# Chunk 0's output as seven block products, and two gate units moved later, to the values of batch 1

The chip is one Trainium2 chip, of which one core is used. The metric is the device time of one execution in microseconds. The kernel before takes 329.07 us (median of three, 328.59 to 329.21; a fourth, the traced one, took 329.17).

## The reference

```python
# q, k, v: (8 batches, 8 heads, 576, 64)
k_p = k.reshape(B, H, 72, 8, D).mean(axis=3)        # keys and values pooled by 8
v_p = v.reshape(B, H, 72, 8, D).mean(axis=3)
attn = softmax(q @ k_p.T / 8)
x = (attn @ v_p) as (4608 tokens, 512)
h = relu(x @ w_gate) * (x @ w_val)                  # (4608, 1536)
out = h @ w_out                                     # (4608, 512)
```

## The kernel before

The 4608 tokens go through in nine chunks of 512. Attention of one batch is woven into the gate and value matmuls of an earlier chunk. A batch has 576 tokens, so chunk 1 needs a rest of batch 0 and four of batch 1's five pieces. Names used below: `a[f]` and `z[f]` are gate and value of the first and second half of chunk 0's tokens; `V[t]` computes piece t of batch 1's values; `x[t]` transposes that piece into `x_T`, the input of the gates; `gv[f]` is a gate and value unit of a later chunk; `kpT0l` and `kpT0u` are the two halves into which a batch's transposed keys are copied, and `px` holds attention values on their way to the transpose. PSUM is the memory in which the results of this kernel's matmuls land; its three pools below hold four, three and one bank, and a pool hands its banks out in turn.

```python
ps_mm  = ctx.enter_context(tc.tile_pool(name="ps_mm", bufs=4, space=PSUM))   # gates, values of w, transposes
ps_at  = ctx.enter_context(tc.tile_pool(name="ps_at", bufs=3, space=PSUM))   # scores, attention values
ps_acc = ctx.enter_context(tc.tile_pool(name="ps_acc", bufs=1, space=PSUM))  # block products
...
def k_transposes(b):
    ps = ps_mm.tile([P, KJ + 1, KROWS], F16, name="mm_ps", tag="mm_ps")
    k_windows(b, ps, 0, KJ + 1)
    eng = nc.scalar if b > 2 else nc.vector
    k_evacuate(b, ps, False, eng)                     # kpT0l
    k_evacuate(b, ps, True, eng)                      # kpT0u
...
def back(b, t, eng):                                  # x[t]
    ...
    for g in range(NG):
        nc.tensor.transpose(out=ps[:, g, :n], in_=x[:, g, :], identity=ident16[:n, :n])
    eng.copy(dst, ps[:, :, :n])                       # into x_T
...
def out_rows(c, ts, eng=None):                        # chunk 0's output, plainly
    cell = []
    def part(lo, hi):
        if not cell:
            cell.append(ps_mm.tile([P, DM], F32, name="mm_ps", tag="mm_ps"))
        for fo in range(lo, hi):                      # 6 matmuls of 512 columns
            nc.tensor.matmul(out=cell[0], lhsT=h_tiles[c][:, fo, ts*P:(ts+1)*P], rhs=wo_sb[:, fo, :], ...)
        ...                                           # after the second half: copy and store
    return [lambda: part(0, n_fo // 2), lambda: part(n_fo // 2, n_fo)]
```

Later chunks use a Strassen-like form (`out_products`): the 2x2 blocks of h and of w_out need seven products in place of eight, for which VectorE makes sums of blocks of h (`sum`) and, once, of w_out (`weight_sums`).

The softmax here doesn't subtract the row's maximum and nothing guards it: scores larger than these inputs give would overflow.

Of the kernel before, what the change touches and what calls it, by code (L numbers as in the profile page):

```python
# [9 lines left out]
F32 = mybir.dt.float32  # L10
# [6 lines left out]
def kernel(  # L17
# [10 lines left out]
    nc = tc.nc  # L28
# [4 lines left out]
    DM = H * D  # L33
    DFF = moe_w_gate.shape[1]
    NTOK = B * S
    P = 128
# [200 lines left out]
    def run(pieces):  # L237
        for piece in pieces:
            piece()
# [26 lines left out]
    def k_transposes(b):  # L266
        ps = ps_mm.tile([P, KJ + 1, KROWS], F16, name="mm_ps", tag="mm_ps")
        k_windows(b, ps, 0, KJ + 1)
        eng = nc.scalar if b > 2 else nc.vector
        k_evacuate(b, ps, False, eng)  # L270
        k_evacuate(b, ps, True, eng)

# [183 lines left out]
        n, j = divmod(t, 2)  # L456
        eng.dma_start(out=out_cols_of[LAST, j, :, n * IQ:(n + 1) * IQ, cols], in_=o)

    def out_rows(c, ts, eng=None):

        cell = []

        def part(lo, hi):
            if not cell:
                cell.append(ps_mm.tile([P, DM], F32, name="mm_ps", tag="mm_ps"))
            t = cell[0]
            for fo in range(lo, hi):
                nc.tensor.matmul(  # L468
                    out=t, lhsT=h_tiles[c][:, fo, ts * P:(ts + 1) * P], rhs=wo_sb[:, fo, :],
                    start=(fo == 0), stop=(fo == n_fo - 1),  # L470
                )
            if hi == n_fo:
                o = fout_pool.tile([P, DM], F32, name="fout")
                if eng is nc.vector:
                    eng.tensor_copy(out=o, in_=t)
                else:
                    nc.scalar.copy(o, t)
                store(o, c * TCH + ts * P)

        return [lambda: part(0, n_fo // 2), lambda: part(n_fo // 2, n_fo)]  # L480



    sends = []
# [14 lines left out]
    def out_products(c, last=False):  # L499


        hc = h_tiles[c]
        a, d1 = hc[:, :n_hf, :HT], hc[:, :n_hf, HT:]
        b, d = hc[:, n_hf:, :HT], hc[:, n_hf:, HT:]
        S = [sum_pool.tile([P, n_hf, HT], F16, name=f"sum{i}") for i in range(4)]
        e, g, h = wo_sb[:, :n_hf, :HD], wo_sb[:, n_hf:, :HD], wo_sb[:, n_hf:, HD:]
        T = [wo_sums[:, i] for i in range(4)]
        p1, u2, u3 = [mid_pool.tile([P, 2, HD], F32, name=f"mid{i}") for i in range(3)]
        rows = [half_pool.tile([P, 2, DM], F32, name=f"rows{i}", bufs=2 - i) for i in range(2)]
        cell = {}  # L510

        def add(k, x, y, op, half):
            i = slice(half * n_hf // 2, (half + 1) * n_hf // 2)
            nc.vector.tensor_tensor(out=S[k][:, i], in0=x[:, i], in1=y[:, i], op=op)  # L514

        def product(lhs, rhs, first):
            if first:
                cell["ps"] = ps_acc.tile([P, 2, HD], F32, name="acc_ps", tag="acc_ps")
            ps = cell["ps"]
            for tb in range(2):  # L520
                for i in range(n_hf):

                    nc.tensor.matmul(  # L523
                        out=ps[:, tb, :], lhsT=lhs[:, i, tb * P:(tb + 1) * P], rhs=rhs[:, i, :],
                        start=(first and tb == 0 and i == 0), stop=(tb == 1 and i == n_hf - 1),
                        skip_group_check=True,
                    )
            return ps

        def plus(out_ap, x, y):  # L530
            nc.vector.tensor_tensor(out=out_ap, in0=x, in1=y, op=ALU.add)  # L531

        def send(half):

            def stores():
                for tb in range(2):
                    store(rows[half][:, tb, :], c * TCH + half * HT + tb * P)

            if c + 2 < n_chunks:
                sends.append(stores)  # L540
            else:
                stores()

        def pr1():
            nc.scalar.copy(p1, product(a, e, True))

        def pr2():
            nc.scalar.copy(rows[0][:, :, :HD], product(b, g, False))

        def pr6():  # L550
            plus(u2, product(S[1], T[1], True), p1)

        def pr7():
            plus(u3, product(S[2], T[2], False), p1)

        def pr4():
            if last:
                plus(rows[1][:, :, :HD], product(d, T[3], True), u3)
                send(1)
            else:  # L560
                plus(rows[1][:, :, :HD], product(d, T[3], False), p1)

        def pr5():
            plus(rows[1][:, :, HD:], product(S[0], T[0], True), u3)
            if not last:
                send(1)

        def pr3():
            plus(rows[0][:, :, HD:], product(S[3], h, False), u2)
            send(0)  # L570

        sums = [lambda k=k, x=x, y=y, op=op, half=half: add(k, x, y, op, half)
                for k, x, y, op in ((0, d1, d, ALU.add), (1, S[0], a, ALU.subtract),
                                    (2, a, d1, ALU.subtract), (3, b, S[1], ALU.subtract))
                for half in range(2)]
        order = [pr1, pr2, pr6, pr7, pr5, pr3, pr4] if last else \
            [pr1, pr2, pr6, pr7, pr4, pr5, pr3]
        return order, sums

    def last_products(c):  # L580
# [292 lines left out]
        trios = [Sc[i:i + 3] for i in range(0, 2 * H, 3)]  # L873
        return [[kt]] + [[]] * (b + 1 < B) + trios + [[p] for p in V], []

    def weave_units(units, others):

        n, m, seq = len(others), len(units), []
        for i, unit in enumerate(units):
            seq += [unit] + others[i * n // m:(i + 1) * n // m]  # L880
        return seq

    with tc.manual_schedule():
        nc.scalar.preload_act_table_set("natural_log_exp_and_others")
        nc.vector.memset(warm_sb, 0.0)
# [52 lines left out]
        half = TCH // 2  # L938
        a = [lambda fo=fo: gate_val(0, fo, 0, half) for fo in range(n_fo)]
        z = [lambda fo=fo: gate_val(0, fo, half, half) for fo in range(n_fo)]  # L940
        o = [p for ts in range(TCH // P) for p in out_rows(0, ts, nc.vector)]
        pv = [lambda half=half: pool_v_array(1, half) for half in range(2)]


# [36 lines left out]
        def kt():  # L981
# [7 lines left out]
        V = [lambda t=t: values(1, t) for t in range(n_pc)]  # L989
        x = [lambda t=t: back(1, t, nc.scalar) for t in range(n_pc)]  # L990

        run([z[3], z[4], z[5], a[6], qt[0], a[7], qt[1], qt[2], kt, z[6], z[7], a[8], *Sc[:4],
             z[8], *Sc[4:6], a[9], *Sc[6:8], z[9], *Sc[8:10], a[10], *Sc[10:12], a[11], *Sc[12:14],
             pv[0], z[10], *Sc[14:], pv[1], z[11], V[4], o[0], V[0], x[4], o[1], V[1], x[0]])
        q_dma(2)
        run([o[2], V[2], x[1], o[3], x[2], V[3], o[4]])
        prep_k(2, True)
        prep_v(2)

# [3 lines left out]
        for c in range(1, n_chunks):  # L1003
            gv = [lambda fo=fo: gate_val(c, fo) for fo in range(n_fo)]

            if c == 1:
                sums = weight_sums()
                units = weave_units(gv[:-1], o[5:])
            elif c < C_HIDDEN:
                prods, sums = out_products(c - 1)  # L1010
                units = []
                order = range(n_fo - 1)
                if c == C_HIDDEN - 1:

                    order = [fo for fo in range(n_fo) if fo % n_hf > 1]
                for fo in order:
                    if c == C_HIDDEN - 1 and len(prods) == 2:
                        units.append(gv[fo])
                        continue
                    units.append(gv[fo])  # L1020
                    if prods and fo not in (1, 4, 7, 10):
                        units.append(prods.pop(0))
            else:
                last = c == n_chunks - 1
                prods, sums = out_products(c - 1, last)
                units = []
                for fo in range(0, n_hf - 2 * last, 2):

                    if sums:
                        mine = [sums.pop(0) for _ in range(4)]  # L1030
                    else:
                        mine = x_sums_of(c + 1)
                    n = 2 if fo else 3
                    units += hidden_round(c, fo, prods[:n], mine)
                    del prods[:n]
                if last:

                    tail, last_sums = [], []

                    def begin_tail():  # L1040
                        products, ready = last_products(c)
                        tail.append(products)
                        last_sums.extend(ready)
                        run(ready[0])

                    units += [gv[n_hf - 2], prods.pop(0), begin_tail,
                              gv[n_fo - 2], lambda: run(last_sums[1]), prods.pop(0),
                              gv[n_hf - 1]]
                else:

                    gv[-1] = lambda: None
# [12 lines left out]
            for i, unit in enumerate(units):  # L1064
# [3 lines left out]
                    prep_v(c + 2)  # L1068
                unit()
                if c == 1:  # L1070
                    run(sums[i:i + 1])
                elif i in SUMS_AT and sums:
                    sums[SUMS_AT.index(i)]()
                if i in (0, 1) and sends:
# [45 lines left out]
```

## Time and profile before

| | before |
|---|---|
| median of three | 329.07 us |
| span of the traced execution | 327.4 us |
| granted TensorE clock | 1.0 |
| TensorE, VectorE, ScalarE, GpSimd busy | 318.7, 226.2, 151.2, 206.9 us |

TensorE is busy for nearly the whole span and makes 89% of the chain that ended last, so this kernel is read by the starts of TensorE's instructions: a group of matmuls that starts later than the last one's columns require has waited. The next two lines are groups by line and form (busy us, mean ns | idle before). They are the two ways of computing the output:

```profile
L468 PE MATMUL mm_ps<-wo_sb,h 128*128 128x512 f16 x48 | 11.7, 379 | 0.0
...
L523 PE MATMUL acc_ps<-wo_sums,sum 128*128 128x256 f16 x252 | 30.9, 272 | 0.0
```

The 48 of L468 are all of chunk 0's output. Their modelled ends overlap: each is listed with 379 ns, but they start 216 ns apart.

### The profile page before, as it was taken

What the parts mean: (1) busy time and instruction counts of PE and PEld (TensorE: products, weight loads), DVE (VectorE), ACT (ScalarE), POOL (GpSimd) and SP (SyncE); (2) the same over time, 40 slices, a digit from 0 to 9 for tenths busy, and PEclk for the clock granted to TensorE, in tenths of its full rate; (3) what the DMA queues carried; (4) which work ended last, traced back from release to release, by engine and by line L of the source; (5) the groups of instructions that cost most, each with busy time, mean ns of one, the idle gap of its engine ahead of it and who ended that gap; (6) DMA issues with size and microseconds to landing.
All of it is one profiled execution on the core that took longest, in us unless ns stands there. A gap on an engine that the chain in (4) does not pass through costs nothing.

```text
span 327.4 us, 7013 instructions
## 1 busy us (share of the span) xinstructions
PE 318.7 (97%) x2670; PEld 226.9 (69%) x2670; DVE 226.2 (69%) x482; ACT 151.2 (46%) x353; POOL 206.9 (63%) x258
## 2 busy tenths in 40 slices
PE   8899999999999999999999999999999999999995
PEld 3577885455566656665898867655667888888674
DVE  7465737677684864696387745784779989879762
ACT  1454482364466226612672257225825565565330
POOL 8556607999999942965199309999901577667300
PEclk9999999999999999999999999999999999999999
DMA  7999998996958538999794472223012130130035
GB/s 110 186 203 202 200 211 151 200 173 118 187 101 159 100 91 86 78 154 160 159 169 76 87 104 60 33 47 124 3 24 50 34 96 2 22 111 2 10 112 137
DMA packets 51010, 35.46 MB, mean 108 GB/s; under 512 B 30432, under 2 KB 45024, under 8 KB 50976
## 3 DMA queue, kind: packets, MB, share of 16 engines
q0 software_dynamic: 18304, 18.88, 36.5%
q1 hardware_dynamic: 32528, 16.00, 26.2%
q8 instruction: 21, 0.34, 0.4%
q10 hardware_dynamic: 144, 0.13, 0.1%
q14 instruction: 13, 0.11, 0.1%
HBM read 37.75 MB, written 9.44 MB: 144 GB/s over the span
## 4 chain that ended last, share of the span: by engine, by line
PE 89%; DVE 6%; DMA 2%; issue 1%; POOL 1%; ACT 0%; DVEq 0%; POOLq 0%
PE mm_ps L430 42%; PE acc_ps L523 19%; PE mm_ps L742 9%; PE at_ps L311 4%; PE mm_ps L468 3%; PE at_ps L389 3%; PE mm_ps L602 2%; DMA q<-in_q_dram 2%; PE at_ps L742 2%; DVE px L395 1%; DVE sum L514 1%; DVE h L439 1%; PE mm_ps L412 1%; PE mm_ps L366 1%; DVE px L758 1%
## 5 line engine op out<-in xcount | busy, mean ns | idle before, releaser
L439 DVE TENSOR_TENSOR h<-mm_ps,relu 128x512 f16<-128x512 f32 (+1 forms) x96 | 59.8, 624 | 69.5 <-PE mm_ps L430 59.2
L436 ACT ACTIVATE relu<-mm_ps 128x512 f16<-128x512 f32 (+1 forms) x96 | 52.2, 544 | 100.1 <-PE mm_ps L430 94.6
L430 PE MATMUL mm_ps<-x_T,wv_sb 128*128 128x512 f16 (+1 forms) x432 | 88.4, 332 | 0.4 <-DVE kpT0u L264 0.4
L430 PE MATMUL mm_ps<-x_T,wg_sb 128*128 128x512 f16 (+1 forms) x432 | 88.5, 331 | 0.0
L430 PEld LDWEIGHTS <-wv_sb 128*128 128x128 f16 x432 | 42.1, 98 | 31.2 <-DVE kpT0u L264 0.8
L430 PEld LDWEIGHTS <-wg_sb 128*128 128x128 f16 x432 | 38.9, 97 | 19.7 <-issue 0.3
L325 ACT ACTIVATE expT<-at_ps 72x288 f16<-72x288 f32 (+2 forms) x128 | 38.8, 374 | 14.3 <-PE at_ps L311 14.2
L523 PEld LDWEIGHTS <-sum 128*128 128x128 f16 x336 | 32.0, 98 | 6.3 <-DVE sum L514 0.9
L395 DVE TENSOR_TENSOR px<-at_ps,prd 128x256 f16<-128x256 f32 (+1 forms) x80 | 33.8, 423 | 2.7
L181 POOL TENSOR_TENSOR tree_b<-tree_a 72x256 f32<-72x256 f32 (+1 forms) x42 | 33.5, 797 | 3.3
L764 POOL TENSOR_TENSOR h<-px 128x256 f16<-128x256 f16 x36 | 25.4, 718 | 13.8 <-ACT px L761 12.8
L175 POOL TENSOR_TENSOR tree_a<-k_in 96x512 f32<-96x512 f16 x18 | 21.5, 1196 | 15.2 <-DMA k_in<-in_k_dram 15.2
L523 PE MATMUL acc_ps<-wo_sums,sum 128*128 128x256 f16 x252 | 30.9, 272 | 0.0
L175 POOL TENSOR_TENSOR tree_a<-v_in 72x512 f32<-72x512 f16 x24 | 28.7, 1197 | 0.1
L523 PEld LDWEIGHTS <-h 128*128 128x128 f16 x252 | 23.7, 98 | 2.9
L763 POOL TENSOR_SCALAR px<-px 128x256 f16<-128x256 f16 x12 | 13.0, 1080 | 18.1 <-PE mm_ps L742 15.3
L844 POOL COPY gate<-h 128x1 f16<-128x1 f16 x4 | 1.5, 380 | 33.9 <-DVE h L439 33.9
L523 PE MATMUL acc_ps<-wo_sb,h 128*128 128x256 f16 x168 | 20.6, 272 | 0.0
L514 DVE TENSOR_TENSOR sum<-h 128x768 f16<-128x768 f16 x28 | 19.0, 679 | 0.0
L531 DVE TENSOR_TENSOR rows<-acc_ps,mid 128x512 f32<-128x512 f32 x21 | 14.4, 686 | 4.7 <-PE acc_ps L523 4.6
L389 PEld LDWEIGHTS <-expT 72*128 72x128 f16 (+1 forms) x280 | 12.9, 100 | 5.9 <-DVE prd L394 0.8
L394 DVE RECIPROCAL prd<-at_ps 128x4 f32<-128x4 f32 (+1 forms) x80 | 13.7, 171 | 3.7 <-PE at_ps L389 3.6
(144 smaller groups left out, 527.9 us busy)
## 6 DMA issues: line engine op xcount, KB each, us to landing
out_dram<-rows SPq DMA_DIRECT2D x24, 256.0 KB
k_in<-in_k_dram POOLq DMA_DIRECT2D x7, 576.0 KB, 7.0
q<-in_q_dram POOLq DMA_DIRECT2D x7, 576.0 KB, 10.0
v_in<-in_v_dram POOLq DMA_DIRECT2D x6, 576.0 KB, 12.7
wg_sb<-in_moe_w_gate_dram POOLq DMA_DIRECT2D x6, 256.0 KB, 11.0
wv_sb<-in_moe_w_val_dram POOLq DMA_DIRECT2D x6, 256.0 KB, 10.8
wo_sb<-in_moe_w_out_dram POOLq DMA_DIRECT2D x3, 512.0 KB, 10.7
v_in<-in_v_dram POOLq DMA_DIRECT2D x2, 512.0 KB, 11.9
```

What stands on the lines that cost most here:

```text
L175: eng.tensor_tensor(out=cell["a"][:n], in0=src[:, :, :4 * D], in1=src[:, :, 4 * D:], op=ALU.add)
L181: eng.tensor_tensor(out=cell["c"][:n], in0=a[:n, :, :2 * D], in1=a[:n, :, 2 * D:], op=ALU.add)
L325: nc.scalar.activation(out=out_ap, in_=in_ap, func=AF.Exp, scale=EXP_SCALE)
L389: nc.tensor.matmul(out=ps[:n, c0:c0 + D + 1], lhsT=weights(b, h, t), rhs=stats[b % 2][:SP, g, s0:s0 + D + 1], start=True, stop=True,)
L395: nc.vector.tensor_tensor(out=x[:n, half * NG // 2:(half + 1) * NG // 2, :, :], in0=pv.rearrange("p g (x c) -> p g x c", x=2)[:, :, :, :D] ...
L430: nc.tensor.matmul(out=t[:, lo:hi], lhsT=w[:, ci, fsl], rhs=x_T[:, ci, x0:x0 + hi - lo], start=(ci == 0), stop=(ci == n_co - 1),)
L436: nc.scalar.activation(out=relu[:, :n], in_=ps[0][:, :n], func=AF.Relu)
L439: nc.vector.tensor_tensor(out=h_tiles[c][:, fo, t0:t0 + n], in0=ps[1][:, :n], in1=relu[:, :n], op=ALU.mult)
L514: nc.vector.tensor_tensor(out=S[k][:, i], in0=x[:, i], in1=y[:, i], op=op)
L523: nc.tensor.matmul(out=ps[:, tb, :], lhsT=lhs[:, i, tb * P:(tb + 1) * P], rhs=rhs[:, i, :], start=(first and tb == 0 and i == 0), stop=(tb ...
L742: nc.tensor.matmul(out=ps[key][:, m], lhsT=w_of(m)[:, i], rhs=xs[:, i], start=(first and m == 0 and i == 0), stop=(m == 1 and i == N_CO - ...
L764: nc.gpsimd.tensor_tensor(out=hc[:, fo_out, cols], in0=gv[:, 0], in1=gv[:, 1], op=ALU.mult)
```

## The change

Chunk 0's output takes the block form as well. As its first two products need only the first half of the tokens (`a`), two units of the second half can come later: `z[10]` just ahead of the first values of batch 1, `z[11]` between them. Half of the weight sums move ahead, and ScalarE copies the keys of batch 2.

```diff
-        eng = nc.scalar if b > 2 else nc.vector
+        eng = nc.scalar
...
-    def out_rows(c, ts, eng=None):                  (removed with its uses)
...
+        if c == 0:
+            order[:2] = [lambda pr=pr, tb=tb: pr((tb,)) for pr in order[:2] for tb in range(2)]
...
+        w_sum = weight_sums()
-             pv[0], z[10], *Sc[14:], pv[1], z[11], V[4], o[0], V[0], x[4], o[1], V[1], x[0]])
+             pv[0], *w_sum[:3], *Sc[14:], pv[1], *w_sum[3:6], z[10], V[4]])
+        prods, sums = out_products(0)
+        run([prods[0], V[0], x[4], prods[1], V[1], x[0], z[11]])
         q_dma(2)
-        run([o[2], V[2], x[1], o[3], x[2], V[3], o[4]])
+        run([prods[2], V[2], x[1], prods[3], V[3], x[2], sums[0]])
...
-                sums = weight_sums()
-                units = weave_units(gv[:-1], o[5:])
+                units = gv[:4] + prods[4:5] + gv[4:6] + prods[5:6] + gv[6:8] + prods[6:7] + \
+                    gv[8:9] + prods[7:8] + gv[9:11] + prods[8:]
+                at = [sums[1:2], sums[2:3], sums[3:4], w_sum[6:7], [w_sum[7], sums[4]],
+                      [w_sum[8], sums[5]], w_sum[9:10], w_sum[10:11], w_sum[11:], [], [], [],
+                      sums[6:7], sums[7:]]            # VectorE sums behind each unit of chunk 1
```

More of the change, by code (lines that the diff above doesn't have):

```diff
@@ L457, in store_cols @@
         eng.dma_start(out=out_cols_of[LAST, j, :, n * IQ:(n + 1) * IQ, cols], in_=o)
-    def out_rows(c, ts, eng=None):
-        cell = []
-        def part(lo, hi):
-            if not cell:
-                cell.append(ps_mm.tile([P, DM], F32, name="mm_ps", tag="mm_ps"))
-            t = cell[0]
-            for fo in range(lo, hi):
-                nc.tensor.matmul(
-                    out=t, lhsT=h_tiles[c][:, fo, ts * P:(ts + 1) * P], rhs=wo_sb[:, fo, :],
-                    start=(fo == 0), stop=(fo == n_fo - 1),
-                )
-            if hi == n_fo:
-                o = fout_pool.tile([P, DM], F32, name="fout")
-                if eng is nc.vector:
-                    eng.tensor_copy(out=o, in_=t)
-                else:
-                    nc.scalar.copy(o, t)
-                store(o, c * TCH + ts * P)
-        return [lambda: part(0, n_fo // 2), lambda: part(n_fo // 2, n_fo)]
     sends = []
@@ L514, in add, with product @@
             nc.vector.tensor_tensor(out=S[k][:, i], in0=x[:, i], in1=y[:, i], op=op)
-        def product(lhs, rhs, first):
-            if first:
+        def product(lhs, rhs, first, blocks=(0, 1)):
+            if first and 0 in blocks:
                 cell["ps"] = ps_acc.tile([P, 2, HD], F32, name="acc_ps", tag="acc_ps")
             ps = cell["ps"]
-            for tb in range(2):
+            for tb in blocks:
                 for i in range(n_hf):
@@ L542, in send, with pr1, pr2 @@
                 stores()
-        def pr1():
-            nc.scalar.copy(p1, product(a, e, True))
-        def pr2():
-            nc.scalar.copy(rows[0][:, :, :HD], product(b, g, False))
+        def pr1(blocks=(0, 1)):
+            ps = product(a, e, True, blocks)
+            if 1 in blocks:
+                nc.scalar.copy(p1, ps)
+        def pr2(blocks=(0, 1)):
+            ps = product(b, g, False, blocks)
+            if 1 in blocks:
+                nc.scalar.copy(rows[0][:, :, :HD], ps)
         def pr6():
@@ L874, in attention @@
         return [[kt]] + [[]] * (b + 1 < B) + trios + [[p] for p in V], []
-    def weave_units(units, others):
-        n, m, seq = len(others), len(units), []
-        for i, unit in enumerate(units):
-            seq += [unit] + others[i * n // m:(i + 1) * n // m]
-        return seq
     with tc.manual_schedule():
@@ L940 @@
         z = [lambda fo=fo: gate_val(0, fo, half, half) for fo in range(n_fo)]
-        o = [p for ts in range(TCH // P) for p in out_rows(0, ts, nc.vector)]
         pv = [lambda half=half: pool_v_array(1, half) for half in range(2)]
@@ L1070 @@
                 if c == 1:
-                    run(sums[i:i + 1])
+                    run(at[i] if i < len(at) else [])
                 elif i in SUMS_AT and sums:
```

## The prediction

> **What bounds the kernel now.** I read the page's busy times first, then the chain that ended last, then the timelines of TensorE, VectorE and ScalarE in the stretch that the change rewrites (45 to 95 us).
>
> ```profile
> PE 318.7 (97%) x2670; PEld 226.9 (69%) x2670; DVE 226.2 (69%) x482; ACT 151.2 (46%) x353; POOL 206.9 (63%) x258
> ...
> PE   8899999999999999999999999999999999999995
> ...
> PE 89%; DVE 6%; DMA 2%; issue 1%; POOL 1%; ACT 0%; DVEq 0%; POOLq 0%
> ```
>
> TensorE is busy in 97% of 327.4 us, at nine tenths or more in every slice but the first two and the last, and it makes 89% of the chain. A microsecond is therefore won only where TensorE streams fewer columns or stands still for less long. The other engines count where TensorE waits for them. The next lines are the chain between batch 0 and chunk 1 (start, length, what):
>
> ```profile
> 56.57 0.22 PE mm_ps L412 x4
> 56.79 0.25 PE at_ps L389 x8
> 57.04 1.30 PE mm_ps L468 x6
> 58.34 1.73 PE mm_ps L430 x8
> ...
> 62.12 0.69 DVE h L439
> 62.81 0.95 DVE wo_sums L494
> 63.76 0.34 DVE kpT0l L264
> 64.10 0.33 issue
> 64.44 0.77 DVE kpT0u L264
> ```
>
> L468 is the old output product of chunk 0, half of one row block in six matmuls: 1.30 us. L430 is a unit of gate and value: eight matmuls, 1.73 us. The DVE pieces are the one place in this stretch where TensorE gives way. VectorE evacuates a gate, makes a weight sum and only then copies the transposed keys out of PSUM, and TensorE wants that bank. The TensorE timeline (start, duration, engine, line, operation, shapes, count, idle time before) shows what it costs:
>
> ```profile
> 56.41 0.39 PE L412 MATMUL mm_ps<-ident,px 128*128 128x128 f16 x4
> 56.63 0.41 PE L389 MATMUL at_ps<-stat,expT 72*128 72x65 f16 x8
> 56.88 1.46 PE L468 MATMUL mm_ps<-wo_sb,h 128*128 128x512 f16 x6
> 58.17 1.03 PE L430 MATMUL mm_ps<-x_T,wg_sb 128*128 128x512 f16 x4
> ...
> 63.88 1.03 PE L430 MATMUL mm_ps<-x_T,wg_sb 128*128 128x512 f16 x4
> 65.26 1.04 PE L430 MATMUL mm_ps<-x_T,wv_sb 128*128 128x512 f16 x4 [0.35 <-DVE kpT0u L264]
> ```
>
> Four such matmuls take 0.865 us from start to start elsewhere, so the second group was due at 64.745 and came at 65.26: 0.515 us lost. (The 0.35 in brackets is less because ends are modelled.) I use starts throughout.
>
> **What the Trainium skill says.** "TensorE: Matmul & The Clock Gate", section "Back-to-back issue gap", gives columns / 2.4 + 2.5 ns for an isolated warm matmul: 215.8 ns at 512 columns, 109.2 at 256. The trace agrees: six of 512 take 1.295 us (215.8 each), and twelve of 256 in the products of later chunks 1.31 us (109.2 each). The same section's lower figure of 131 ns for sustained 512-column matmuls is not seen. Its paragraph on engine queue depths (section "Architectural detail: the array is 16× 32×32, not 1× 128×128") calls VectorE's and ScalarE's queues strict first in, first out; that is why a copy queued behind a gate and a sum comes late, which the DVE lines above show. "GPSIMD Engine Reference", section "1. Specifications", says that GpSimd's SBUF interfaces are shared with VectorE and contended when a VectorE instruction has two SBUF inputs. The weight sums agree: 0.42 us at best, up to 1.11 us while GpSimd pools keys and values.
>
> **The change part by part.**
>
> 1. *Fewer columns.* Removed: 48 matmuls of 512 columns, 8 halves x 1.295 = 10.36 us. Added: 7 products of 12 matmuls of 256 columns, 7 x 1.31 = 9.17 us. All on TensorE, all on the path: **-1.19 us**.
>
> 2. *Keys of batch 2 copied by ScalarE.* A later batch's two such copies took 0.63 us each on ScalarE. ScalarE idles 1.43 us before the gate at 63.21, and the keys are ready about 62.3, so the bank is free about 63.6, before 64.745. The wait goes: **-0.515 us**.
>
> 3. *Added work beside TensorE.* VectorE gets eight sums of 128x768 (0.55 us alone, a median of 1.02 for those that read a sum and h; some 6.4 us at 0.8) and five adds out of PSUM (0.69), and loses four 0.69 us output copies and two key copies (1.5). Six of twelve weight sums move ahead to 46 to 48.5 us, where GpSimd idles, so they should run near 0.42. Net some +4 us of VectorE spread over 40 us in which it is about 70% busy. ScalarE gets two 0.59 us copies. None lies on the path by itself. The last of the output weights lands at 35.1 + 12.5 = 47.6 us, about when the fifth weight sum wants it: just in time.
>
> 4. *The shorter filling between the values of batch 1.* Before, five halves of 1.295 us stood between the values (L389), their transposes (L412) and chunk 1. Now there are four halves of a product (0.655 each) and one gate unit (0.88). VectorE's work for one values unit (two reciprocals, two multiplications) takes 1.1 us and follows this pace:
>
> ```profile
> 49.50 0.42 DVE L439 TENSOR_TENSOR h<-mm_ps,relu 128x256 f16<-128x256 f32 x1 [1.49 <-PE mm_ps L430]
> 49.84 0.16 DVE L394 RECIPROCAL prd<-at_ps 64x4 f32<-64x4 f32 x1
> 50.04 0.42 DVE L395 TENSOR_TENSOR px<-at_ps,prd 64x256 f16<-64x256 f32 x1
> 50.38 0.17 DVE L394 RECIPROCAL prd<-at_ps 64x4 f32<-64x4 f32 x1
> 50.58 0.42 DVE L395 TENSOR_TENSOR px<-at_ps,prd 64x256 f16<-64x256 f32 x1
> ```
>
> The first values unit started at 49.32 on TensorE; its result is finished at 51.00, 1.68 us later. With half a product in place of a full half, the transpose wants it after 0.38 + 0.655 + 0.25 = 1.29 us and gets it about 1.74: **+0.43 us** with the small slip of the second values unit. The transposes of the next two lose 0.05 to 0.1 together, and the last one (x[2]) comes right after its values V[2], one half product and V[3], and loses about 0.2: **+0.3 us**.
>
> 5. *The join to chunk 1.* Chunk 1's first gate reads the columns of x_T that x[2] writes. Before, x[2] at 56.41 had V[3] and a full half behind it (0.25 + 1.295 us), and its copy was done in time:
>
> ```profile
> 56.83 0.59 ACT L414 COPY x_T<-mm_ps 128x512 f16<-128x512 f16 x1 [0.93 <-PE mm_ps L412]
> ```
>
> From the start of the transpose to the end of the copy is 57.42 - 56.41 = 1.01 us. In the changed order only a vector sum follows x[2]; the next TensorE work is that gate. The transposes take 0.22 us, so TensorE stands for 1.01 + 0.06 - 0.22: **+0.85 us**. 0.06 is my estimate for a semaphore's way.
>
> Sum: -1.19 - 0.515 + 0.43 + 0.3 + 0.85 = **-0.1 us**. The work moves (this stretch ends some 2.5 us sooner, chunk 1 has 6.55 in place of 3.885 us of output work), but nearly all that is saved comes back as waits.
>
> **Rivals.**
>
> *The arithmetic gain survives* (-1.7 us, 327.4). It would if the waits of 4 and 5 were covered. For it: the unit order puts z[11] before V[2], so VectorE may be less behind than I think. Against: nothing in the diff stands between x[2] and the first gate, and that wait follows from the data.
>
> *VectorE becomes the limit* (+1 to +2 us, 330 to 331). The first summed product needs four sums, one behind each of four gate evacuations, and the next product needs two more beside weight sums, while GpSimd is over 90% busy (18.9 of 20 us from 60 to 80). By my count the sums end 0.2 to 0.3 us before TensorE asks. Chunk 1's products already showed such a wait once, of under 0.5 us. Against: VectorE idles 0.8 to 1.8 us before many gates.
>
> *The stores become the limit.* 1 MB moves from 53 to 87 us to the start of chunk 2. Against: no TensorE wait on a DMA is seen after the start, and nothing on TensorE needs a store. With the first store gone ahead of it, the transposing DMA of batch 2's queries may even start earlier. Worth about nothing.
>
> **Range and chances.** The sum says 329.0; the term most likely too big is the waits in 4, so I lean a little to the gain: **328.6 us**. Low end 327.4: the full arithmetic gain. High end 329.8: my waits plus 0.8 us of waits for sums. The three runs of before spread 0.6 us, which adds little. 2% is 6.6 us, more than all that is touched here can give: within 2% 0.98, faster 0.01, slower 0.01.
>
> **What would show it.** No L468 rows; twelve-matmul products of 1.31 us in their place, two split in halves of 0.655. The key copies of batch 2 on ScalarE, and no TensorE wait on kpT0u. A TensorE gap of 0.7 to 1 us before the first 512-column gate of chunk 1, released by the ScalarE copy of x_T, and one of about 0.4 us before the first transpose of batch 1, released by VectorE's px. Chunk 1's first gate at about 55.7 us (58.17 before). It would be wrong if TensorE shows none of these gaps (then 327.4), or if the first or second summed product waits for sums by over 0.3 us, or if the scores of batch 2 wait for their queries, wanted some 3 us sooner than before.

## The result

The changed kernel takes 329.6 us (median of four, 329.06 to 329.63). Ratios here are the mean time of one kernel's runs over that of the other's runs of the same rounds, so not quite the ratio of the medians quoted. Executions over 1.5% slower than the fastest of the same kernel are left out of the means. Against before it is 1.0014, interval 0.9997 to 1.0031: within 2%, and no difference that can be told from noise. The traced execution spans 327.3 us (before 327.4). It is the shortest of the four: the others span 327.8 to 327.9 and have no trace, so the account below is that of the shortest one.

The page of the changed kernel (busy times; then the chain by engine):

```profile
PE 317.5 (97%) x2706; PEld 230.2 (70%) x2706; DVE 230.2 (70%) x489; ACT 153.5 (47%) x357; POOL 207.5 (63%) x258
...
PE 88%; DVE 6%; DMA 2%; ACT 1%; issue 1%; POOL 1%; DVEq 0%; ACTq 0%; POOLq 0%
```

TensorE has 36 matmuls more (84 in place of 48) and 1.2 us less to do, and ScalarE appears in the chain with 1%. TensorE's timeline at the join to chunk 1 and in chunk 1 shows where the saving went:

```profile
49.90 0.54 PE L412 MATMUL mm_ps<-ident,px 64*128 64x64 f16 x4
50.37 0.83 PE L500 MATMUL acc_ps<-wo_sb,h 128*128 128x256 f16 x6
...
54.16 0.41 PE L389 MATMUL at_ps<-stat,expT 72*128 72x65 f16 x8
54.41 0.48 PE L412 MATMUL mm_ps<-ident,px 128*128 128x128 f16 x4
55.56 1.02 PE L430 MATMUL mm_ps<-x_T,wg_sb 128*128 128x512 f16 x4 [0.67 <-ACT x_T L414]
...
61.27 1.03 PE L430 MATMUL mm_ps<-x_T,wg_sb 128*128 128x512 f16 x4
62.13 1.03 PE L430 MATMUL mm_ps<-x_T,wv_sb 128*128 128x512 f16 x4
...
69.34 1.68 PE L500 MATMUL acc_ps<-wo_sums,sum 128*128 128x256 f16 x12
70.86 0.29 PE L311 MATMUL at_ps<-qT,kpT0l 128*72 128x288 f16 x1
```

At 49.90 the four transposes of x[4] take 0.47 us to the next group; before, they took 0.22. The 0.25 us lost between them is a wait for VectorE's `px`. Before, x[2] had 1.55 us of TensorE work behind it. Now the four transposes of x[2] at 54.41 take 0.22 us and the gate follows only at 55.56: 0.93 us lost, to the ScalarE copy into x_T. At 62.13 the value matmuls of chunk 1's fourth unit come on time; before, they came 0.515 us late. At 69.34 a product takes 1.52 us to the next group where twelve such matmuls take 1.31: 0.21 us lost in its middle. The chain (start, length, what) tells why the gate came when it did:

```profile
53.67 0.67 PE acc_ps L500 x6
54.34 0.02 issue
54.36 0.59 ACT rows L529
54.95 0.58 ACT x_T L414
55.52 0.04 issue
55.56 1.89 PE mm_ps L430 x8
```

The copy of the second product stands ahead of the copy of x_T in ScalarE's queue. That adds only about 0.1 us, because x[2] is not finished much sooner.

A landmark in both kernels is the group of seven key transposes of batch 3 near the start of chunk 2. It starts at 89.07 us before and at 88.81 after, so the rewritten stretch gains 0.26 us. By starts: -1.19 for the columns, -0.515 for the wait on the keys, +0.93 before the gate, +0.25 in x[4], +0.21 in the product at 69.34: -0.3 us. In chunk 2 another 0.18 us goes: a score matmul at 95.14 waits for a PSUM bank that VectorE empties late. At the last key transposes, 226.05 before, the gain is 0.09 us.

### The profile page after: what moved, and what is told of

It is laid out like the page before. It is cut to its first block, busy times and chain, and to the rows that moved or that the text cites. A ratio compares the mean times of both kernels' runs of the same rounds, so it can differ in the third digit from the quotient of the medians.

```text
span 327.3 us, 7099 instructions
## 1 busy us (share of the span) xinstructions
PE 317.5 (97%) x2706; PEld 230.2 (70%) x2706; DVE 230.2 (70%) x489; ACT 153.5 (47%) x357; POOL 207.5 (63%) x258
## 4 chain that ended last, share of the span: by engine, by line
PE 88%; DVE 6%; DMA 2%; ACT 1%; issue 1%; POOL 1%; DVEq 0%; ACTq 0%; POOLq 0%
PE mm_ps L430 42%; PE acc_ps L500 22%; PE mm_ps L726 9%; PE at_ps L311 4%; PE at_ps L389 3%; PE mm_ps L586 2%; DVE px L395 2%; DMA q<-in_q_dram 2%; PE at_ps L726 2%; DVE sum L491 1%; DVE h L439 1%; DVE px L742 1%; PE mm_ps L412 1%; PE mm_ps L282 1%; PE mm_ps L342 1%
## 5 line engine op out<-in xcount | busy, mean ns | idle before, releaser
L500 PEld LDWEIGHTS <-sum 128*128 128x128 f16 x384 | 36.5, 98 | 7.3 <-DVE sum L491 1.2
L500 PE MATMUL acc_ps<-wo_sums,sum 128*128 128x256 f16 x288 | 35.5, 272 | 0.0
L500 PEld LDWEIGHTS <-h 128*128 128x128 f16 x288 | 27.0, 98 | 3.3
L500 PE MATMUL acc_ps<-wo_sb,h 128*128 128x256 f16 x192 | 23.9, 272 | 0.0
L491 DVE TENSOR_TENSOR sum<-h 128x768 f16<-128x768 f16 x32 | 22.8, 712 | 0.0
L508 DVE TENSOR_TENSOR rows<-acc_ps,mid 128x512 f32<-128x512 f32 x24 | 16.5, 687 | 5.3 <-PE acc_ps L500 5.1
```

Of the source, the lines that this page charges most:

```text
L491: nc.vector.tensor_tensor(out=S[k][:, i], in0=x[:, i], in1=y[:, i], op=op)
L500: nc.tensor.matmul(out=ps[:, tb, :], lhsT=lhs[:, i, tb * P:(tb + 1) * P], rhs=rhs[:, i, :], start=(first and tb == 0 and i == 0), stop=(tb ...
```

## The experiments

Eleven runs were made. The traces settle what a wait costs. Whole executions of one kernel differ by up to 1 or 2 us, so totals are quoted with their range, and the start of a trace is allowed for (the same early group starts up to 0.25 us apart from one trace to another). The expectations count the runs in the order below.

### Run 1: the kernel before with the keys on ScalarE

```diff
-        eng = nc.scalar if b > 2 else nc.vector
+        eng = nc.scalar
```

> The kernel before with one line changed: ScalarE copies the keys of batch 2. Theory (TensorE's stream sets the time, and each wait counts in full): the wait for kpT0 before the value matmuls of chunk 1's fourth unit goes, the key transposes of batch 3 move from 89.07 to about 88.55 us, and the span falls by 0.5 us. Rival (a later stretch is bound by another engine and absorbs what is won here): the wait goes but the span stays within 0.1 us of 327.4.

The wait is gone. The key transposes of batch 2, ahead of the edit, start at 62.02 (before 61.85); those of batch 3 at 88.71 (before 89.07): 0.53 us gained, as expected. The last matmul group starts at 321.55 against 321.89, so with the late start of 0.17 us the gain is still 0.51 us at the end. The span is 327.0. Fast runs took 328.81 to 329.42 (a fifth, 333.88 us, is slow and has no trace); ratio 0.9994, 0.9975 to 1.0014: too small for the totals to show.

### Run 2: the changed kernel with z[11] behind x[2]

```diff
-        run([prods[0], V[0], x[4], prods[1], V[1], x[0], z[11]])
+        run([prods[0], V[0], x[4], prods[1], V[1], x[0]])
...
-        run([prods[2], V[2], x[1], prods[3], V[3], x[2], sums[0]])
+        run([prods[2], V[2], x[1], prods[3], V[3], x[2], z[11], sums[0]])
```

> The changed kernel with the last gate unit of chunk 0 (z[11]) moved from before the third product half to behind the transpose x[2]. Theory (the gate of chunk 1 waits 0.9 us only because nothing stands behind x[2]): the gap at 55.56 us goes; the transposes x[1] and x[2], which now come 0.9 us sooner, wait 0.1 to 0.3 us each for px, so chunk 1 begins its first gate 0.4 to 0.7 us sooner than in the changed kernel and the span falls as much, to about 326.8. Rival one (the wait is for something else, such as the store or the copy of the products): the gap stays at about 0.9 us. Rival two (VectorE's pace sets this stretch): the first gate of chunk 1 comes no sooner, the same time is lost before x[1] and x[2].

TensorE's timeline of this run:

```profile
54.10 0.48 PE L412 MATMUL mm_ps<-ident,px 128*128 128x128 f16 x4
54.41 0.60 PE L430 MATMUL mm_ps<-x_T,wg_sb 128*128 128x256 f16 x4
54.85 0.60 PE L430 MATMUL mm_ps<-x_T,wv_sb 128*128 128x256 f16 x4
55.29 1.03 PE L430 MATMUL mm_ps<-x_T,wg_sb 128*128 128x512 f16 x4
...
69.07 0.49 PE L500 MATMUL acc_ps<-wo_sums,sum 128*128 128x256 f16 x3
70.29 1.16 PE L500 MATMUL acc_ps<-wo_sums,sum 128*128 128x256 f16 x9 [0.74 <-DVE sum L491]
```

The gap before the gate is gone: the unit fills it and the gate follows at 55.29 without a pause. That is 0.27 us sooner than in the changed kernel, or 0.47 with the 0.2 us by which this trace starts late. The rest was not lost to `px` before x[1] and x[2], as I had expected, but 0.36 us before the third product half (52.07), which waits for ScalarE's copy of the first product. But the key transposes of batch 3 start at 89.23, later than the 88.81 of the changed kernel. The gain was lost at the second summed product, which does three matmuls and then waits for a VectorE sum. The theory of the gap holds; that of the whole stretch had left out a second limit behind the first. The traced execution is the longest of six (328.19 to 329.7; ratio 0.9986, 0.9966 to 1.0005); whether the shorter ones lose less there was not traced.

### Run 3: the changed kernel with the keys back on VectorE

```diff
-        eng = nc.scalar
+        eng = nc.scalar if b > 2 else nc.vector
```

> The changed kernel with the key copies of batch 2 back on VectorE. Theory (the copies on ScalarE take a wait of about half a microsecond off the path): TensorE waits for kpT0 again, 0.5 us or somewhat more as VectorE now has the sums too, and the span rises by 0.5 to 1.0 us. Rival (the wait was already gone with the shifted weight sums): span unchanged within 0.1 us.

TensorE's timeline of this run; the last line is from VectorE's:

```profile
61.42 1.03 PE L430 MATMUL mm_ps<-x_T,wg_sb 128*128 128x512 f16 x4
62.28 1.03 PE L430 MATMUL mm_ps<-x_T,wv_sb 128*128 128x512 f16 x4
63.14 0.29 PE L311 MATMUL at_ps<-qT,kpT0l 128*72 128x288 f16 x1
...
61.62 0.76 DVE L264 COPY kpT0u<-mm_ps 64x576 f16<-64x576 f16 x1
```

The wait does not come back: the value matmuls start 0.86 us after the gate's, on time, while VectorE copies the second keys from 61.62 to 62.38. From batch 2's keys (59.39, changed kernel 59.24) to batch 3's (88.92, changed kernel 88.81) the two kernels differ by 0.04 us. Times 329.18 to 330.32, ratio to before 1.0019 (0.9999 to 1.004). The theory fell: in the changed kernel the choice of the engine is worth nothing, though in the kernel before it is worth 0.5 us. The run alone does not say why. VectorE is also less late here: its copy ends 0.10 us after the value matmuls are due (62.38 against 62.28), where before it ended 0.455 us after (65.20 against 64.745), because the sum ahead of it took 0.66 us in place of 1.03. So the rival of my expectation, the shifted weight sums, could explain most of it. Run 8 separates the two.

### Run 4: both gate units moved

```diff
-             pv[0], *w_sum[:3], *Sc[14:], pv[1], *w_sum[3:6], z[10], V[4]])
+             pv[0], *w_sum[:3], *Sc[14:], pv[1], *w_sum[3:6]])
...
-        run([prods[0], V[0], x[4], prods[1], V[1], x[0], z[11]])
+        run([prods[0], V[4], prods[1], V[0], x[4], z[10], V[1], x[0]])
...
-        run([prods[2], V[2], x[1], prods[3], V[3], x[2], sums[0]])
+        run([prods[2], V[2], x[1], prods[3], V[3], x[2], z[11], sums[0]])
```

> The changed kernel with another order between the values of batch 1: the first half product ahead of the first values, the gate unit z[10] in the middle, z[11] behind x[2]. Theory (the waits of this stretch come only from what stands between values and transpose, and between transpose and gate): both the wait of about 0.25 us before x[4] and the 0.93 us before chunk 1 go, 0.2 to 0.4 us come back before x[1] and x[2]; span 326.4 to 326.8, 0.5 to 0.9 us under the changed kernel. Rival (VectorE's pace sets the stretch, some 1.1 us for each values unit): no gain over the changed kernel, the waits move to x[0] to x[2].

The first gate of chunk 1 starts at 54.81, 0.75 us sooner than in the changed kernel. The wait in x[4] falls from 0.25 to 0.14 us, and 0.32 us comes back in x[1], as expected. Again what was won is lost in the second summed product, which waits 0.81 us, and the key transposes of batch 3 start at 88.82. VectorE's timeline of this run ahead of that product:

```profile
64.75 1.37 DVE L471 TENSOR_TENSOR wo_sums<-wo_sb 128x512 f16<-128x512 f16 x1
66.04 1.08 DVE L491 TENSOR_TENSOR sum<-h 128x768 f16<-128x768 f16 x1
67.04 0.68 DVE L439 TENSOR_TENSOR h<-mm_ps,relu 128x512 f16<-128x512 f32 x1
67.64 1.18 DVE L471 TENSOR_TENSOR wo_sums<-wo_sb 128x512 f16<-128x512 f16 x1
68.74 1.08 DVE L491 TENSOR_TENSOR sum<-h 128x768 f16<-128x768 f16 x1
```

VectorE stands in a row of operations, of which those with two inputs in SBUF (the on-chip memory that holds h and the weights) take 1.08 to 1.37 us where the same ones take 0.41 to 0.55 elsewhere; the multiplication that reads PSUM takes its usual 0.68. GpSimd pools the next batch at that time. TensorE's product starts at 68.58; its last sum ends at 69.8. The six executions fall in two groups, 327.64 to 327.88 (three) and 329.24 to 329.83 (three); the traced one is of the longer group. Ratio 0.9978 (0.9953 to 1.0002). What separates the groups was not traced.

### Run 5: added work on TensorE

```diff
+                gv[9] = lambda f=gv[9]: (warm(6), f())
```

> The changed kernel with six useless matmuls of 512 columns (1.30 us, zeros) ahead of chunk 1's tenth gate unit, at about 80 us, after all waits of this stretch. Theory (TensorE's stream carries what is won or lost here to the end): the key transposes of batch 4 and the end come 1.3 us later, span 328.6 and time 330.5 to 331. Rival (a later stretch is paced by another engine and absorbs shifts): the shift shrinks under 0.7 us by the end.

The added matmuls stand for 1.3 us. The last product group ahead of them starts 0.26 us later than in the changed kernel (79.09 against 78.83). The key transposes of batch 3 start at 90.36, 1.55 us later, and the last matmul group at 324.16, 2.35 us later. Nothing was absorbed; two waits for VectorE were added (0.51 us recorded at 119.15 and 0.35 at 153.92). The times are 330.67 to 332.72, ratio to before 1.0057 (1.0033 to 1.0082). So time lost in this stretch is lost at the end. That the traced execution overshoots was not expected, and half of the executions, at 330.67 to 330.77, do not.

### Run 6: both units, and the second summed product one unit later

```diff
 (the edits of run 4, and)
-                units = gv[:4] + prods[4:5] + gv[4:6] + prods[5:6] + gv[6:8] + prods[6:7] + \
+                units = gv[:4] + prods[4:5] + gv[4:7] + prods[5:6] + gv[7:8] + prods[6:7] + \
```

> The order of the fourth run (both gate units moved), and the second summed product of chunk 0 one gate unit later. In the fourth run the 0.8 us won before chunk 1 was lost again: that product waited 0.81 us in its middle for a VectorE sum. Theory (two limits in a row: first the copy of x_T, then VectorE's sums beside GpSimd): with one unit more in between the wait for the sum goes and the gain stays; span 326.2 to 326.7, some 0.8 us under the fourth run and about 1.0 under the changed kernel. Rival (VectorE is over-full in this whole stretch): the wait of 0.8 us moves to a later product.

The key transposes of batch 3 start at 88.02 and the last group at 320.75, 0.79 and 1.06 us sooner than in the changed kernel (0.93 and 1.20 with the late start of 0.14 us); the span is 326.3. Between 50 and 90 us TensorE no longer waits for a sum. That is what the theory of two limits in a row says, and what is won stays won to the end. But two of six executions took 331.67 and 332.91 us; the other four 328.05 to 328.73. The ratio is 1.002 with an interval of 0.9974 to 1.0066.

### Run 7: the product later, alone

> The changed kernel with only the second summed product one gate unit later. Theory: its wait there is only about 0.2 us, because chunk 1 began 0.9 us late; so only 0.2 us is won, span about 327.1. Rival (VectorE's sums are the one limit and the gap before chunk 1 costs nothing): 0.5 us or more is won, and the run with both is no better.

The edit is the second one of run 6. In chunk 1 it does what the theory said: the wait in the product is gone and batch 3's keys start at 88.49, 0.32 us sooner (0.22 with the early start of this trace). The total is a miss: 329.49 to 332.22 us, ratio 1.0043 (1.0013 to 1.0072). The trace shows another wait, in chunk 4:

```profile
155.91 0.60 PE L430 MATMUL mm_ps<-x_T,wg_sb 128*128 128x256 f16 x4
159.59 0.61 PE L430 MATMUL mm_ps<-x_T,wg_sb 128*128 128x256 f16 x4 [3.08 <-DMA x_T<-px]
```

A transposing DMA that brings values of batch 3 into x_T is late. The issues of the five such DMAs from the sync engine stretch over 15.5 us (140.92 on) against 8.2 in the first trace of the changed kernel and 11.2 in its second (run 9), where TensorE does not wait. Runs 9 to 11 ask whether this belongs to the edit.

### Run 8: the kernel before with one output block in its own bank

```diff
-                cell.append(ps_mm.tile([P, DM], F32, name="mm_ps", tag="mm_ps"))
+                pool, name = (ps_acc, "acc_ps") if ts == 2 else (ps_mm, "mm_ps")
+                cell.append(pool.tile([P, DM], F32, name=name, tag=name))
```

> The kernel before with its third output block (o[4] and o[5], whose halves stand 10 us apart) accumulated in the idle accumulation bank in place of one of the four banks that gates, values and transposes share; keys still copied by VectorE. Theory two (the key copies were waited for because the half-finished product holds one of the four banks, so three were left): the wait of 0.5 us at 65.26 us goes and the span falls by 0.5 us, although VectorE copies as late as before. My first theory (the copies are late behind a gate and a sum in VectorE's queue, whatever the banks): the wait stays at about 0.5 us.

TensorE's timeline of this run; the last line is from VectorE's:

```profile
63.81 1.03 PE L430 MATMUL mm_ps<-x_T,wg_sb 128*128 128x512 f16 x4
64.67 1.03 PE L430 MATMUL mm_ps<-x_T,wv_sb 128*128 128x512 f16 x4
...
82.04 0.30 PE L389 MATMUL at_ps<-stat,expT 72*128 72x65 f16 x4 [0.45 <-DVE px L395]
...
64.58 0.76 DVE L264 COPY kpT0u<-mm_ps 64x576 f16<-64x576 f16 x1
```

The value matmuls come 0.86 us after the gate's, on time, although VectorE copies the second keys as late as before (64.58 to 65.34, so until 0.67 us after these matmuls have begun; before 64.44 to 65.20). So the wait was one for a bank. A plain output block stood half done in one of the four shared banks for 10 us, between o[4] at 56.88 and o[5] at 66.52; with three banks left, the matmuls needed the one with the keys. "Perfetto Trace Analysis", section "Matmuls" (under "Optimizing Tensor Performance"), says that independent groups should rotate through different banks so that emptying one overlaps the next group's matmuls; here one group that pauses takes a bank out of that rotation, and the trace agrees with 0.515 us. The rest of my expectation missed: the span stayed at 327.4, because another wait came at 82.04, for a bank of values that VectorE empties (0.45 us recorded, 0.61 by starts). A weight sum ahead of that work took 1.44 us at 79.98, where the same one took 0.68 in run 1 (80.22), which kept its gain. The times are 328.53 to 329.23 and one slow run; ratio 0.9987 (0.9969 to 1.0004).

### Run 9: the changed kernel again

> The changed kernel once more, unaltered, for more executions and a second trace. Its four executions so far spanned 327.3 to 327.9 us and the traced one was the shortest. Theory (the second summed product waits for VectorE's sums by an amount that follows the phase of GpSimd's pooling): spans of 327.3 to 328.3, and a longer span goes with a longer wait in that product (0.2 us in the first trace). Rival: the longer executions have a wait for a DMA in chunk 3 or 4, none in that product.

Five executions span 327.1 to 328.0 us (328.85 to 329.8; ratio to before 1.001, 0.9998 to 1.0022). The traced one, at 327.2, has the same waits: the gate of chunk 1 at 55.54 (recorded idle 0.67) and the product of twelve at 69.32 with 1.71 us. As it was again one of the shorter, what the longer ones have was not seen: inconclusive on that point.

### Run 10: run 6 again

> The order of the sixth run once more. Two of its six executions took 331.7 and 332.9 us, 3 to 4 us over the others, and the traced execution of the run with only the product moved waited 3.08 us for a transposing DMA of x_T at the start of chunk 4. Theory (with the summed product one unit later, chunk 2 starts sooner, its DMA traffic meets the stores of chunk 0, and in some executions the backlog reaches chunk 4): again at least one of six executions over 331 us, the others near 328.3. Rival (chance): none in six.

No execution over 331 us: 327.76 to 329.39, mean 328.65, against 328.93 of before in the same rounds (ratio 0.9997, 0.9985 to 1.001, by paired rounds) and 329.24 of the changed kernel on the same chip. The trace spans 326.0 us. Its join to chunk 1 and its two summed products:

```profile
53.85 0.60 PE L430 MATMUL mm_ps<-x_T,wg_sb 128*128 128x256 f16 x4
54.29 0.60 PE L430 MATMUL mm_ps<-x_T,wv_sb 128*128 128x256 f16 x4
54.72 1.03 PE L430 MATMUL mm_ps<-x_T,wg_sb 128*128 128x512 f16 x4
...
62.54 1.47 PE L500 MATMUL acc_ps<-wo_sums,sum 128*128 128x256 f16 x12
70.48 1.47 PE L500 MATMUL acc_ps<-wo_sums,sum 128*128 128x256 f16 x12
```

No gap and two products without a pause: the key transposes of batch 3 start at 87.75 and the last matmuls at 320.48, 1.33 us sooner than in the changed kernel. With its early start of 0.12 us the gain is 0.94 us at batch 3's keys and 1.21 at the end, within 0.01 us of run 6. The long executions did not return.

### Run 11: run 6 with the stores of chunk 0 later

```diff
-                if i in (0, 1) and sends:
+                if i in ((7, 8) if c == 2 else (0, 1)) and sends:
```

> As the sixth run, with the stores of chunk 0 (1 MB) issued behind units 8 and 9 of chunk 2 in place of 1 and 2, so that they leave the queue free for the transposing DMA of the queries. Theory (the stores of chunk 0 start the backlog): no execution over 331 us, all near 328.3, and the queries' transpose at about 93 us issues in 3 us or less in place of 4.6 to 5.3. Rival (the backlog comes from the loads and transposes alone): long executions as often as in the run without this edit.

Two of six executions were long (336.56 and 331.6 us), the other four 328.13 to 328.75; ratio 1.0005 (0.9975 to 1.0035). The queries' transpose at 92.63 does issue in 2.70 us, as expected, but long executions came as often as in run 6. In the traced one, the long one, TensorE waits 4.82 us before a gate at 161.59, and the transposes into x_T are issued over 17.3 us. The profile puts this wait down to a store; a gate reads no stored rows, and the weight load of the same line waited 5.1 us for the transposing DMA. So stores of chunk 0 at their old place are not needed for it. What makes chunk 4 wait for a transposing DMA in some executions stays open. The wait was seen in two of the four traces with the second summed product moved, and in none of the others. Of all executions with it moved (runs 6, 7, 10 and 11) 7 of 24 took over 331 us. Of the others, without run 5, 2 of 64 did: one each of runs 1 and 8 (333.88 and 338.29 us), whose kernels have no such product. So it looks as if the edit makes them more frequent, but they exist without it, and no run shows how the one leads to the other.

## Why the prediction was right, point by point

The time lies in the range, near its upper end, and the forecast that the difference stays within 2% held. The sum of -0.1 us before I leaned towards the gain is also what the traced spans show, but that is partly luck: item 4 was 0.5 us too large, and items 3 and 5 together 0.5 us too small.

1. *Columns, -1.19 us.* Right. Twelve matmuls of 256 columns take 1.31 us in the new products too.
2. *Keys, -0.515 us.* The size is right (the wait is absent), the reason is wrong. I read it as VectorE copying late. Run 3 shows that VectorE may copy in the changed kernel at no cost, and run 8 that in the kernel before the wait goes with the bank, however late the copy. The seven products work in ps_acc and so free the fourth shared bank; the move to ScalarE would have been enough alone (run 1), but adds nothing to it.
3. *Work beside TensorE, free.* Wrong by some tenths. I had put it among the rivals that VectorE's sums might be late and then counted that they end 0.2 to 0.3 us before they are asked for. The second summed product waited 0.21 us in the trace, and a bank for scores in chunk 2 came 0.18 us later. (The terms listed there, +6.4 and +3.45 for sums and adds, -2.76 and -1.5 for copies, make +5.6 us of VectorE, not 4. The page shows +4.0, so that figure was right although its list does not give it; six weight sums did get faster, 0.36 us each between 46.0 and 48.1 us.) Behind a chunk 1 that starts sooner the first of these grows to 0.74 and 0.81 us (runs 2 and 4).
4. *Waits among the values, +0.43 and +0.3 us.* Right in kind, mis-sized: 0.25 us in x[4], for `px` as predicted, and next to nothing before the others. z[11] gave VectorE time there: where it stands behind x[2] (run 4), 0.32 us comes back in x[1].
5. *Join to chunk 1, +0.85 us.* Right: 0.93 us, released by the copy of x_T as predicted, and removed by runs 2, 4, 6 and 10. Some 0.1 us of it is the copy of the second product ahead in ScalarE's queue, which I had left out. Chunk 1's first gate was put at 55.7 us and came at 55.56.

The rival in which stores limit something found no support. The lean of 0.4 us to the gain was wrong: the medians lie 0.2 to 0.5 us over those of before, within noise. Why three of the first four executions of the changed kernel span 0.5 us more than the traced one stays open.

So the saving of 1.7 us was real on TensorE and was turned into new waits: 0.9 us for ScalarE's copy (item 5), 0.25 us for VectorE's values (item 4) and 0.2 to 0.4 us for its sums and a bank (item 3). The traces of runs 6 and 10 show that reordering wins 1.2 us of it back in good executions. Neither is clearly faster than the kernel before in total, so no version here is shown to beat both.

## What to carry to other kernels

When filler between a producer and its consumer gets shorter, count again what stands behind each copy: here one transpose with nothing behind it cost three quarters of the arithmetic saved. A gap that is filled hands the time to the next deadline, so look at what the engine beside has to deliver next before counting the gain. A wait that names a copying engine may be one for a buffer that something else has held for long, so ask who owns the other buffers.

## What the Trainium skill lacked or had wrong

- "TensorE: Matmul & The Clock Gate", "Back-to-back issue gap", gives about 131 ns for each 512-column matmul in a sustained stream with weight loads. Here such streams start 215.8 ns apart; its formula for isolated matmuls (215.8 and 109.2 ns at 512 and 256 columns) is what holds.
- "GPSIMD Engine Reference", "1. Specifications", names the contention of GpSimd with VectorE operations of two SBUF inputs and gives no size. Nor does "SBUF — State Buffer" give a time for such shapes. Beside GpSimd's pooling, the 128x512 fp16 subtractions of run 4 took 1.18 to 1.37 us in place of 0.41, and the 128x768 sums 1.08 in place of 0.55. That GpSimd is the cause is read from the timing alone; no run took its work away.
- None of the pages read says how far the issue of one transposing DMA may stretch: into x_T it took 1.19 us as a rule, and up to 8.07 us in the traced execution of run 7, with TensorE waiting 3.08 us.
